# Scaling and splitting the value matrix of later batches on ScalarE and GpSimd, one fold for two column maxima, and another order of evictions near the last query block

## The chip, the cores and the metric

The kernel runs on one core of a Trainium2 chip. The metric is device time in microseconds (us). Engines as the profile names them: PE (TensorE, matrix products), PEld (its weight loads), DVE (VectorE), ACT (ScalarE), POOL (GpSimd), SP (SyncE, here only a DMA queue). Each engine executes its own instruction list in order and waits on semaphores of the others.

## The reference

Two layers run one after the other, all in float32.

1. Attention over pooled keys. For each of 4 batches, `kv` (384 x 32 positions, 128 channels) is averaged over 4 x 4 patches to 768 rows and multiplied with `w_sr`; the result is both `k` and `v`. For 12288 queries per batch: `s = q k^T / sqrt(128)`, softmax over the 768 keys, output `a v`.
2. A soft mixture of experts over all 49152 rows `x` of that output: `logits = x phi` (32 slots); a softmax over all rows (per slot) gathers slot inputs, 8 experts (128 to 1024 to 128, ReLU) map them, and a softmax over slots (per row) spreads the slot outputs back over the rows.

The queries and `phi` are scaled by 200, so the products need nearly full float32 accuracy: operands are split into a high and a low part and multiplied in several passes.

## The kernel before

**Tiling.** The queries are cut into 96 blocks of 512, 24 blocks per batch. For one block: `q_hi` (ACT, L448) and `q_lo` (POOL, L452) split the queries; `qk` (PE, L462 to L464) makes the scores of 768 keys in three PSUM pairs of banks (s0 to s2); `rowmax1` to `rowmax4` (DVE L469, L479, L481, a PE product L489, DVE L494, L499) find the row maximum and spread it; `sub` (DVE, L507) subtracts it and so frees the score banks; `exp_hi` and `exp_t` (ACT, L514, L518) make the exponentials as f16 and as f32; `plo` (POOL L523, on DVE for the last block) makes the low part of the f16 split; `av_hi` and `av_lo` (PE, L540, L541, L548) multiply with the value matrix; `av_evac` (L556 on DVE for block 94, the last but one, L558 on ACT for the others) moves the result out of one of two PSUM banks called m. Groups of 4 blocks then feed the softmax over rows of the second layer (`g0` to `g7a`, L582 to L685).

**The value matrix.** It is not `v` alone: `w_sb` holds `w_sr` and `w_sr phi` beside each other, so the matrix has 128 + 32 columns, and the logits come out of the same product. For each batch, `kv_ops` prepares it: `kv_k_*` (keys, split in two), `kv_v_mm` and `kv_v_out` (values, f32, tile `v32`), `kv_m` (DVE: largest absolute value in each row, for two halves h of the keys and for two column ranges k, 128 and 32 columns wide, L377; then L382 joins the halves), `kv_d` (ACT: puts those on a diagonal, L386), `kv_s_mm` and `kv_s_g` (PE and DVE: largest value over all rows, rounded down to a power of two, and its inverse), `kv_t_hi` (ACT L418: scaled values as f16, tile `vhi`), `kv_t_lo` (DVE: L425 sets the ones column of `vhi`, L426 makes `vlo = v * inv - vhi` in one instruction with two inputs in SBUF). For batch 0 this runs at the start; for batches 1 to 3 it runs in the last third of the batch before, between ordinary blocks.

**Order.** The order of all instructions on PE, DVE, ACT and POOL is written by the class `Plan`, a list scheduler. Each `op` gets an engine, an assumed cost, a priority (a planned time, smallest first), dependencies and the rings (tiles, PSUM banks) that it acquires and releases. `emit` simulates the engines with these assumed costs and calls the functions in simulated order; the chip's engines then keep that order, however long things really take. `PER` (9.8 us) is the assumed period of a block; the preparation of the next batch starts at the priority of `KV0` = 14.5 blocks after block 2 of a batch, and its steps lie `KVS` block periods apart. An `op` that releases a bank m gets 60 off its priority, so it comes first once it is ready. The plan assumed `dve(768) + 0.06` = 0.93 us and `dve(192) + 0.06` = 0.33 us for the two `kv_t_lo`.

**End.** After block 95, the last groups (L612 to L685), the experts (`t_psi` to `t_so`), the product `t_q` (L1063, PSUM bank m, tile `psq`) with its split `t_shi` and `t_slo`, and then chunks of output: `c_t`, `c_hi`, `c_lo` (a transposition through a bank m and its split), `o_mm`, `o_ev`, `o_dma`. The low parts of block 95 (`plo`, DVE) and the evictions of block 94 (`av_evac`, DVE) lie close together on DVE there.

Of the kernel before, what the change touches and what calls it, by code (L numbers as in the profile page):

```python
# [9 lines left out]
F32 = mybir.dt.float32  # L10
# [161 lines left out]
def attention_then_soft_moe(ctx: ExitStack, tc: tile.TileContext, qT, kv0, kvT, w_sr, w_srT, phi, w1, w2, outT):  # L172
# [112 lines left out]
    KVS = 0.9  # L285
# [84 lines left out]
    def kv_m(b, k, h):  # L370
        if k == 0 and h == 0:
            AM[b] = (
                bp.tile([P, 4], F32, tag="am", name=f"am_{b}", bufs=1),
                bp.tile([P, 2, P], F32, tag="dg", name=f"dg_{b}", bufs=1),
            )
        am = AM[b][0]
        nc.vector.tensor_reduce(  # L377
            out=am[:, 2 * h + k : 2 * h + k + 1], in_=VU[b][:, 3 * h : 3 * h + 3, VSRC[k]], axis=XY, op=ALU.max,
            apply_absolute_value=True,
        )  # L380
        if h:
            nc.vector.tensor_tensor(out=am[:, k : k + 1], in0=am[:, k : k + 1], in1=am[:, 2 + k : 3 + k], op=ALU.max)  # L382
# [25 lines left out]
    def kv_t_hi(b, k):  # L408
# [9 lines left out]
        nc.scalar.activation(hi[:, :, src.start + 1 : src.stop + 1], v[:, :, src], AF.Copy, scale=inv[:, k : k + 1])  # L418
# [131 lines left out]
    def av_evac(i, k):  # L550
# [4 lines left out]
        if i == NB - 2:  # L555
# [238 lines left out]
    def kv_ops(b, base, step, dep0, dep1):  # L794
# [11 lines left out]
        for h in range(2):  # L806
# [78 lines left out]
    def av_rest(i, k, m, p, prev):  # L885
        los = [ops["lo", i, 0], ops["lo", i, 1]]
        a2 = op("PE", 6 * 0.072, 0.17, p + 0.8, prev + los, lambda: av_lo(i, k), use=[("plo", (i, 0)), ("plo", (i, 1)), m])
        if k % 2:
# [4 lines left out]
                "DVE" if i == NB - 2 else "ACT", act(2 * VW) + (0.1 if i == NB - 2 else -0.03), 0.1, p - 2, [a2] + evs[-1:], lambda: av_evac(i, k // 2),  # L893
# [323 lines left out]
```

## Time and profile before

| what | value |
|---|---|
| median of 3 runs | 1143.38 us (1140.43 to 1143.49) |
| the profiled execution's own time | 1142.69 us |
| its span, first to last instruction | 1140.9 us |
| busy: PE, DVE, POOL, ACT | 1059.1, 1007.6, 860.3, 821.7 us |
| mean granted TensorE clock | 0.973 |

How to read it: busy time is a sum over an engine's instructions. In the lists of instructions a row gives start (us), duration (us), engine, line, operation and shapes, and in brackets the idle time just before it and what ended that. In lists of waits, a row gives who waited for whom, us in total, how often, and the longest. Rows of windows give, for a stretch of time, each engine's busy time with its instructions, the granted clock (PEclk), the DMA share and GB/s. L numbers are lines of the kernel before.

### The profile page before, as it was taken

How to read it: one execution, taken by the hardware profiler on the slowest of the kernel's cores; microseconds unless marked ns; L12 is line 12 of the kernel's file. 1: busy time of each engine (PE TensorE's matmuls, PEld its weight loads, DVE VectorE, ACT ScalarE, POOL GpSimd, SP SyncE). 2: the span in 40 equal slices, each digit the busy share in tenths (PEclk: the TensorE clock that was granted, in tenths of full speed). 3: DMA queues.
4: the chain of work that ended last, by engine and by line, in shares of the span. 5: the costliest groups of instructions: out<-in, count | busy, mean ns of one | idle time of the engine just before them, and what ended most of it. 6: DMA issues, size and time to landing. Idle time of an engine off the chain costs nothing.

```text
span 1140.9 us, 24642 instructions
## 1 busy us (share of the span) xinstructions
PE 1059.1 (93%) x10198; PEld 905.7 (79%) x10198; DVE 1007.6 (88%) x1506; ACT 821.7 (72%) x999; POOL 860.3 (75%) x471
## 2 busy tenths in 40 slices
PE   3799999998999999998999999998999999997785
PEld 2588888887888888887888888887888888886342
DVE  7889888999889988999989989999989988986895
ACT  1678778776777878776877788786788777874564
POOL 0678889777899889777889888868889889772430
PEclk9899999998999999999999999999999999998976
DMA  9225320120126310120136210210110110113398
GB/s 351 96 47 126 94 56 1 38 93 1 38 57 128 86 52 2 41 90 1 38 82 123 66 52 1 76 55 1 39 38 1 38 38 2 38 38 111 136 388 361
DMA packets 17406, 89.14 MB, mean 78 GB/s; under 512 B 1680, under 2 KB 3984, under 8 KB 11152
## 3 DMA queue, kind: packets, MB, share of 16 engines
q1 hardware_dynamic: 13408, 69.47, 16.4%
q0 software_dynamic: 3312, 17.70, 8.2%
q8 instruction: 81, 1.33, 0.5%
q10 hardware_dynamic: 576, 0.41, 0.1%
q14 instruction: 29, 0.24, 0.1%
HBM read 58.87 MB, written 25.17 MB: 74 GB/s over the span
## 4 chain that ended last, share of the span: by engine, by line
PE 63%; DVE 28%; issue 3%; ACT 2%; POOL 2%; DMA 1%; DVEq 0%; SPq 0%; POOLq 0%; ACTq 0%
PE m L540 10%; PE m L541 10%; PE m L548 9%; PE s L462 9%; DVE t L507 8%; PE s L464 8%; PE s L463 8%; DVE r L469 8%; PE m L489 3%; PE m L679 2%; DVE mb L499 2%; DVE o L1111 1%; POOL plo L523 1%; DVE cm L617 1%; PE po L1102 1%
## 5 line engine op out<-in xcount | busy, mean ns | idle before, releaser
L523 POOL TENSOR_TENSOR plo<-t,phi 128x1536 f16<-128x1536 f32 x190 | 595.4, 3144 | 153.8 <-ACT t L518 152.6
L514 ACT ACTIVATE phi<-t,lnk 128x1536 f16<-128x1536 f32 x192 | 301.0, 1570 | 120.2 <-DVE t L507 118.6
L469 DVE TRANSPOSE_TENSOR_REDUCE r<-s 128x32 f32<-128x1024 f32 x288 | 350.8, 1236 | 29.2 <-PE s L464 23.4
L540 PE MATMUL m<-vhi,phi 128*128 128x161 f16 x2280 | 358.3, 235 | 3.5 <-DVE acc L685 2.9
L541 PE MATMUL m<-vlo,phi 128*128 128x160 f16 x2280 | 357.5, 234 | 0.0
L507 DVE TENSOR_TENSOR t<-s,mb 128x1024 f32<-128x1024 f32 (+1 forms) x384 | 343.2, 951 | 8.2
L518 ACT ACTIVATE t<-t,lnk 128x1536 f32<-128x1536 f32 x192 | 299.7, 1568 | 2.8
L540 PEld LDWEIGHTS <-phi 128*128 128x128 f16 x2304 | 228.2, 99 | 24.7 <-issue 24.7
L462 PE MATMUL s<-qhi,khi 128*128 128x512 f32 x576 | 239.0, 415 | 5.8 <-DVE t L507 5.7
L541 PEld LDWEIGHTS <-phi 128*128 128x128 f16 x2304 | 226.7, 98 | 5.4 <-issue 3.9
L464 PE MATMUL s<-qhi,klo 128*128 128x512 f32 x576 | 229.3, 398 | 0.1
L463 PE MATMUL s<-qlo,khi 128*128 128x512 f32 x576 | 228.8, 397 | 0.0
L548 PE MATMUL m<-vhi,plo 128*128 128x161 f16 x2280 | 227.9, 235 | 0.2 <-POOL plo L523 0.2
L548 PEld LDWEIGHTS <-plo 128*128 128x128 f16 x2304 | 179.8, 101 | 2.6 <-issue 1.2
L558 ACT ACTIVATE xl<-m 128x322 f32<-128x322 f32 x188 | 81.0, 431 | 105.0 <-PE m L548 100.5
L452 POOL TENSOR_TENSOR qlo<-q,qhi 128x512 fp32r<-128x512 f32 x96 | 125.9, 1312 | 26.8 <-ACT qhi L448 26.8
L462 PEld LDWEIGHTS s<-qhi,khi 128*128 128x128 f32 x576 | 109.5, 190 | 29.8 <-issue 4.1
L464 PEld LDWEIGHTS s<-qhi,klo 128*128 128x128 f32 x576 | 109.1, 189 | 26.9 <-DVE klo L353 0.5
L463 PEld LDWEIGHTS s<-qlo,khi 128*128 128x128 f32 x576 | 109.6, 190 | 22.4 <-issue 0.7
L499 DVE STREAM_TRANSPOSE mb<-m 128x512 f32<-128x512 f32 x96 | 68.3, 711 | 3.3
L448 ACT ACTIVATE qhi<-q 128x512 fp32r<-128x512 f32 x96 | 59.1, 617 | 2.4 <-PE s L464 1.1
L489 PE MATMUL m<-rq,sel 128*128 128x64 f32 x192 | 40.5, 293 | 19.9 <-DVE rq L481 19.9
(136 smaller groups left out, 842.4 us busy)
## 6 DMA issues: line engine op xcount, KB each, us to landing
q<-qT SPq DMA_DIRECT2D x23, 1024.0 KB, 4.8
outT<-o SPq DMA_DIRECT2D x21, 1024.0 KB, 6.2
kva<-kvT POOLq DMA_DIRECT2D x9, 1536.0 KB, 11.6
kva<-kvT SPq DMA_DIRECT2D x3, 1536.0 KB, 10.2
kv<-kv SPq DMA_DIRECT2D x8, 512.0 KB, 5.7
w<-w SPq DMA_DIRECT2D x2, 1536.0 KB, 6.4
w<-w SPq DMA_DIRECT2D x4, 768.0 KB, 4.2
outT<-o SPq DMA_DIRECT2D x6, 512.0 KB, 6.2
```

Of the source, the lines that this page charges most:

```text
L452: nc.gpsimd.tensor_tensor(out=lo, in0=q_src(i), in1=hi.bitcast(F32), op=ALU.subtract)
L462: nc.tensor.matmul(s, khi[:, ks], hi, start=True, stop=False)
L463: nc.tensor.matmul(s, khi[:, ks], lo, start=False, stop=False)
L464: nc.tensor.matmul(s, klo[:, ks], hi, start=False, stop=True)
L469: nc.vector.tensor_reduce(out=MX[i][:, 2 * u : 2 * u + 2, :].rearrange("p t b -> p (t b)"), in_=S[i, u].rearrange("p t (b j) -> p (t b) j" ...
L507: nc.vector.tensor_tensor(out=TT_[i, h][:, o : o + n, :], in0=S[i, t // 2][:, u : u + n, :], in1=MX[i].unsqueeze(1).broadcast_to([P, n, BQ ...
L514: nc.scalar.activation(hi, TT_[i, h], AF.Exp, bias=lnk, scale=SCALE)
L518: nc.scalar.activation(t, t, AF.Exp, bias=lnk, scale=SCALE)
L523: eng.tensor_tensor(out=lo, in0=TT_.pop((i, h)), in1=PP[i, h], op=ALU.subtract)
L540: nc.tensor.matmul(px, p, vhi[:, t, :], start=(t == 0), stop=False)
L541: nc.tensor.matmul(px[:, 1:], p, vlo[:, t, :], start=False, stop=False)
L548: nc.tensor.matmul(px, PP[i, t // TH][1][:, t % TH, ks], vhi[:, t, :], start=False, stop=(t == NT - 1))
```

## The change

- `kv_m`: the four maxima lie as `[k, h]` in one tile, and one `tensor_reduce` over h writes both joined maxima to a new tile `am2`; the two `tensor_tensor` instructions of L382 go. `kv_d` reads `am2`, and both of its instructions come after all maxima.
- `kv_t_hi`, batches 1 to 3: ACT scales `v` in place (f32), then copies it to f16, two instructions in place of one for each column range. Batch 0 keeps its one.
- `kv_t_lo`, batches 1 to 3: POOL subtracts (`vlo = v - vhi`, v being scaled by now) and sets the ones column. Batch 0 keeps DVE.
- `av_evac` of block 94: its first half (query columns 0 to 255) stays on DVE, its second half goes from DVE to ACT. In the plan, the low parts of block 95 on DVE depend on that first half, so that it is written ahead of them.
- `t_q`: `psq` lies in the score banks s1 in place of a bank m.
- `KVS` from 0.9 to 1.0, and the plan's costs follow the new instructions.

```diff
-    KVS = 0.9
+    KVS = 1.0
...
-                bp.tile([P, 4], F32, tag="am", name=f"am_{b}", bufs=1),
+                bp.tile([P, 2, 2], F32, tag="am", name=f"am_{b}", bufs=1),
                 bp.tile([P, 2, P], F32, tag="dg", name=f"dg_{b}", bufs=1),
+                bp.tile([P, 2], F32, tag="am2", name=f"am2_{b}", bufs=1),
...
-            out=am[:, 2 * h + k : 2 * h + k + 1], in_=VU[b][:, 3 * h : 3 * h + 3, VSRC[k]], axis=XY, op=ALU.max,
+            out=am[:, k, h : h + 1], in_=VU[b][:, 3 * h : 3 * h + 3, VSRC[k]], axis=XY, op=ALU.max,
...
-        if h:
-            nc.vector.tensor_tensor(out=am[:, k : k + 1], in0=am[:, k : k + 1], in1=am[:, 2 + k : 3 + k], op=ALU.max)
+        if h and k:
+            nc.vector.tensor_reduce(out=am2, in_=am, axis=X, op=ALU.max)
...
-        nc.scalar.activation(dg[:, k, :], ident, AF.Copy, scale=am[:, k : k + 1])
+        nc.scalar.activation(dg[:, k, :], ident, AF.Copy, scale=am2[:, k : k + 1])
...
-        nc.scalar.activation(hi[:, :, src.start + 1 : src.stop + 1], v[:, :, src], AF.Copy, scale=inv[:, k : k + 1])
+        part = hi[:, :, src.start + 1 : src.stop + 1]
+        if b:
+            nc.scalar.activation(v[:, :, src], v[:, :, src], AF.Copy, scale=inv[:, k : k + 1])
+            nc.scalar.activation(part, v[:, :, src], AF.Copy)
+        else:
+            nc.scalar.activation(part, v[:, :, src], AF.Copy, scale=inv[:, k : k + 1])
...
+        if b:
+            if k == 0:
+                nc.gpsimd.memset(hi[:, :, :1], 1.0)
+            nc.gpsimd.tensor_tensor(out=lo[:, :, src], in0=v[:, :, src], in1=hi[:, :, src.start + 1 : src.stop + 1], op=ALU.subtract)
+            return
...
-        if i == NB - 2:
+        if i == NB - 2 and k == 0:
             nc.vector.tensor_copy(XL[g][:, o : o + 2, :], PX.pop((i, k)))
         else:
             nc.scalar.activation(XL[g][:, o : o + 2, :], PX.pop((i, k)), AF.Copy)
...
-            ops["lo", i, h] = op("DVE" if i == NB - 1 else "POOL", 1.67 if i == NB - 1 else 3.1, 0.1, T0 + 9 + 3.2 * h, [e2], lambda i=i, h=h: plo(i, h), acq=[("plo", (i, h))], use=[("t", (i, h)), ("phi", (i, h))])
+            ops["lo", i, h] = op(
+                "DVE" if i == NB - 1 else "POOL", 1.67 if i == NB - 1 else 3.1, 0.1, T0 + 9 + 3.2 * h,
+                [e2] + ([ops["x", NB - 2, 0]] if i == NB - 1 else []), lambda i=i, h=h: plo(i, h),
+                acq=[("plo", (i, h))], use=[("t", (i, h)), ("phi", (i, h))],
+            )
...
-            a = op("ACT", act(n, 1), 0.1, base + step * (6 + k), prev, lambda k=k: kv_t_hi(b, k), use=[("v32", b)])
-            ops["t", b, k] = op("DVE", dve(n) + 0.06, 0.08, base + step * (6 + k), [a], lambda k=k: kv_t_lo(b, k), use=[("v32", b)])
+            a = op("ACT", act(n, 1) * (2 if b else 1), 0.1, base + step * (6 + k), prev, lambda k=k: kv_t_hi(b, k), use=[("v32", b)])
+            ops["t", b, k] = op("POOL" if b else "DVE", 2.1 * n / 1000 + 0.3 if b else dve(n) + 0.06, 0.08, base + step * (6 + k), [a], lambda k=k: kv_t_lo(b, k), use=[("v32", b)])
...
-        W["psq"] = mt([P, 512], "psq")
+        W["psq"] = ps.tile([P, 2, 512], F32, tag="s1", name="psq")[:, 0, :]
```

More of the change, by code (lines that the diff above doesn't have):

```diff
@@ L372, in kv_m @@
             AM[b] = (
-                bp.tile([P, 4], F32, tag="am", name=f"am_{b}", bufs=1),
+                bp.tile([P, 2, 2], F32, tag="am", name=f"am_{b}", bufs=1),
                 bp.tile([P, 2, P], F32, tag="dg", name=f"dg_{b}", bufs=1),
+                bp.tile([P, 2], F32, tag="am2", name=f"am2_{b}", bufs=1),
             )
-        am = AM[b][0]
+        am, _, am2 = AM[b]
         nc.vector.tensor_reduce(
-            out=am[:, 2 * h + k : 2 * h + k + 1], in_=VU[b][:, 3 * h : 3 * h + 3, VSRC[k]], axis=XY, op=ALU.max,
+            out=am[:, k, h : h + 1], in_=VU[b][:, 3 * h : 3 * h + 3, VSRC[k]], axis=XY, op=ALU.max,
             apply_absolute_value=True,
         )
-        if h:
-            nc.vector.tensor_tensor(out=am[:, k : k + 1], in0=am[:, k : k + 1], in1=am[:, 2 + k : 3 + k], op=ALU.max)
+        if h and k:
+            nc.vector.tensor_reduce(out=am2, in_=am, axis=X, op=ALU.max)
     def kv_d(b, k):
-        am, dg = AM[b]
-        nc.scalar.activation(dg[:, k, :], ident, AF.Copy, scale=am[:, k : k + 1])
+        _, dg, am2 = AM[b]
+        nc.scalar.activation(dg[:, k, :], ident, AF.Copy, scale=am2[:, k : k + 1])
     def kv_s_mm(b):
@@ L812, in kv_ops @@
             for k in range(2):
-                m[k].append(op("DVE", (0.53 if k == 0 else 0.2) + 0.2 * h, 0.08, p + step * (1 + 0.4 * k), [at_["vo", h]] + m[k] + m[0][:1], lambda h=h, k=k: kv_m(b, k, h), use=[("v32", b)]))
-        d = [op("ACT", 0.25, 0.1, base + step * 5, m[k], lambda k=k: kv_d(b, k)) for k in range(2)]
+                m[k].append(op("DVE", (0.53 if k == 0 else 0.2) + 0.2 * h * k, 0.08, p + step * (1 + 0.4 * k), [at_["vo", h]] + m[k] + m[0][:1], lambda h=h, k=k: kv_m(b, k, h), use=[("v32", b)]))
+        d = [op("ACT", 0.4, 0.1, base + step * 5, m[0] + m[1], lambda k=k: kv_d(b, k)) for k in range(2)]
         s = op("PE", 0.6, 0.4, base + step * 5.5, d, lambda: kv_s_mm(b), acq=[("m", ("pa", b))])
@@ L892, in av_rest @@
             ops["x", i, k // 2] = op(
-                "DVE" if i == NB - 2 else "ACT", act(2 * VW) + (0.1 if i == NB - 2 else -0.03), 0.1, p - 2, [a2] + evs[-1:], lambda: av_evac(i, k // 2),
+                "DVE" if i == NB - 2 and k == 1 else "ACT", act(2 * VW) + (0.1 if i == NB - 2 and k == 1 else -0.03), 0.1, p - 2, [a2] + evs[-1:], lambda: av_evac(i, k // 2),
                 acq=[x] if first else [], use=[m] + ([] if first else [x]),
@@ L1148, in attention_then_soft_moe @@
         sq.append(tail("DVE", 1.05, [a] + sq, lambda h=h: t_so(h), use=[sk]))
-    a = tail("PE", 0.4, sq[1:], t_q, acq=[("m", "psq")])
-    shi = tail("ACT", 0.25, [a, qt], t_shi, use=[("m", "psq")])
-    slo = tail("DVE", 0.3, [shi], t_slo, use=[("m", "psq")])
+    a = tail("PE", 0.4, sq[1:], t_q, acq=[("s1", "psq")])
+    shi = tail("ACT", 0.25, [a, qt], t_shi, use=[("s1", "psq")])
+    slo = tail("DVE", 0.3, [shi], t_slo, use=[("s1", "psq")])
     for g in range(len(GB)):
```

## The prediction

> **What bounds the kernel now.** I read the page's busy times first, then the windows of equal length, then the waits of PE by stretch, and at last the lists of instructions around each wait.
>
> ```profile
> span 1140.9 us, 24642 instructions
> PE 1059.1 (93%) x10198; PEld 905.7 (79%) x10198; DVE 1007.6 (88%) x1506; ACT 821.7 (72%) x999; POOL 860.3 (75%) x471
> ```
>
> PE is the bound, DVE close behind. The average hides stages. Windows (columns: length, busy time and instructions of PE, PEld, DVE, ACT, POOL, clock, DMA):
>
> ```profile
> 313.70:342.20 28.50, 28.30 (x299) 24.92 (x297) 25.52 (x39) 21.10 (x25) 26.22 (x15) 1.00 0.30 57
> 256.70:285.20 28.50, 24.70 (x218) 22.19 (x216) 26.13 (x36) 18.54 (x24) 20.06 (x11) 0.88 0.01 1
> 770.00:798.60 28.60, 23.87 (x246) 20.85 (x245) 26.32 (x40) 18.96 (x24) 22.95 (x14) 1.00 0.00 1
> ```
>
> An ordinary window has PE busy throughout (28.30 of 28.50). The windows near the end of a batch, where the value matrix of the next one is prepared, have 24.70 and 23.87. PE time lost there is never made up, since PE has no slack elsewhere. What PE waited for, in the stretches 245 to 300 (the one from 500 to 560 reads the same), 755 to 815 (two rows), 196 to 257 (450 to 513 and 700 to 771 read the same), and last, for comparison, 795 to 1027, about 22 ordinary blocks:
>
> ```profile
> PE m L489 <- DVE rq L481: 3.8, 2, 3.1
> ...
> PE m L489 <- DVE rq L481: 4.4, 2, 3.1
> PE s L462 <- DVE t L507: 0.4, 1, 0.4
> ...
> PE m L679 <- DVE m L494: 1.0, 1, 1.0
> ...
> PE m L489 <- DVE rq L481: 0.9, 5, 0.2
> ```
>
> In 22 blocks together PE waits 0.9 us for the row maximum, and 3.1 us at once in each preparation. Why DVE is late there, with batch 0's two instructions of the same kind last:
>
> ```profile
> 255.67 3.12 POOL L523 TENSOR_TENSOR plo<-t,phi 128x1536 f16<-128x1536 f32 x1 [3.31 <-ACT t L518]
> 257.27 2.34 DVE L426 SCALAR_TENSOR_TENSOR vlo<-v,inv,vhi 128x768 f16<-128x768 f32 x1
> 259.99 3.09 POOL L523 TENSOR_TENSOR plo<-t,phi 128x1536 f16<-128x1536 f32 x1 [1.20 <-ACT t L518]
> 260.80 2.49 DVE L426 SCALAR_TENSOR_TENSOR vlo<-v,inv,vhi 128x192 f16<-128x192 f32 x1
> 263.93 0.66 PE L489 MATMUL m<-rq,sel 128*128 128x64 f32 x2 [3.12 <-DVE rq L481]
> 33.47 1.01 DVE L426 SCALAR_TENSOR_TENSOR vlo<-v,inv,vhi 128x768 f16<-128x768 f32 x1
> 34.40 0.41 DVE L426 SCALAR_TENSOR_TENSOR vlo<-v,inv,vhi 128x192 f16<-128x192 f32 x1
> ```
>
> The two instructions of L426 took 1.01 and 0.41 us at the start, where POOL ran nothing, and 2.34 and 2.49 beside `plo`. Each ends just after the POOL instruction beside it (258.79, 263.08), 0.8 and 0.2 us later. The small one is six times its own length. The plan had counted 0.93 and 0.33, so the order it wrote puts PE's row-maximum product 4.83 - 1.26 = 3.6 us too early, and PE stands for 3.1.
>
> **The price of the wait goes on in the clock.** After it PE runs slowly for a while (windows of 3 us):
>
> ```profile
> 264.00:267.00 3.00, 3.00 (x22) 3.00 (x23) 2.23 (x4) 0.00 (x0) 1.43 (x2) 0.50 0.00 0
> 267.00:270.00 3.00, 3.00 (x17) 2.71 (x15) 2.96 (x5) 2.78 (x3) 0.00 (x0) 0.52 0.00 0
> ...
> 518.00:521.00 3.00, 1.82 (x13) 1.85 (x14) 1.99 (x6) 0.00 (x0) 2.68 (x3) 0.67 0.00 0
> 521.00:524.00 3.00, 3.00 (x26) 2.86 (x24) 3.00 (x4) 1.63 (x2) 0.00 (x0) 0.76 0.00 0
> ```
>
> At clock 0.50 and 0.52 PE loses 3 x 0.50 + 3 x 0.48 = 2.9 us. In the second preparation it loses 3 x 0.33 + 3 x 0.24 = 1.7. In the third the clock stayed at 1.00 (window above): 4.6 us in all.
>
> **The change, part by part.**
>
> *Low parts and folds leave DVE.* Per later batch DVE loses both L426 (4.83 us) and both folds of L382, and gets one reduction over 4 numbers:
>
> ```profile
> L382 DVE TENSOR_TENSOR am<-am x8: 160/498/1506, 28.0 to 746.2; 128x1 f32<-128x1 f32 x8
> L619 DVE TENSOR_REDUCE cmt<-cm 128x1 f32<-128x16 f32 x23 | 3.9, 170 | 0.8
> ```
>
> L382 also has two SBUF inputs and takes 0.16 alone, up to 1.51 beside POOL. One such fold stands between PE's product L489 and L494, for which L679 then waits 1.0 us. The reduction has one input: nearest row 0.17, bounds 0.15 and 1.5 if it were held as well; I take 0.17, the mean of 23 of them, most of which ran while POOL was busy (it is 75% of the span). So the waits to go are 3.8 + 3.8 + 4.4 + 0.4 = 12.4, 3 x 1.0 = 3.0 and the clock's 4.6: 20.0 us. The Trainium skill, SBUF — State Buffer, section "SBUF: two separate sides", says that VectorE and GpSimd share a pair of ports as an exclusive lock for a whole instruction, and that on VectorE two SBUF inputs are enough to need it; by that rule the fold costs 0.17, without it up to 3 x 1.3 = 4 us of DVE would remain. The stretched L426 and L382 agree with it.
>
> *ACT and POOL get it.* The nearest rows:
>
> ```profile
> L418 ACT ACTIVATE vhi<-v,inv 128x768 f16<-128x768 f32 x4 | 3.7, 930 | 1.5 <-DVE inv L403 1.5
> L418 ACT ACTIVATE vhi<-v,inv 128x192 f16<-128x192 f32 x4 | 1.8, 444 | 0.0
> L523 POOL TENSOR_TENSOR plo<-t,phi 128x1536 f16<-128x1536 f32 x190 | 595.4, 3144 | 153.8 <-ACT t L518 152.6
> L227 POOL MEMSET sm<- 128x256 f32 x1 | 0.3, 315 | 0.0
> 270.89 3.13 POOL L523 TENSOR_TENSOR plo<-t,phi 128x1536 f16<-128x1536 f32 x1 [5.45 <-ACT t L518]
> ```
>
> ACT gets 0.93 + 0.44 = 1.37 us more per batch, and each copy waits for the scaling just ahead of it. Behind them on ACT stand exponentials and evictions, for which POOL's `plo` and PE's two m banks wait. POOL gets 3144 x 960 / 1536 = 1.97 us plus at most 0.32 for the ones column: 2.3. Behind it stand `plo` and `qlo`, for which PE waits. The cover: ACT is idle 7.4 us of the ordinary 28.5 above, and POOL waited 5.45 us for ACT near this place; the value matrix itself is needed some three blocks later. Bounds for both together: 0 (covered), and without cover all of it, 1.37 + 2.3 = 3.7 us per batch, 11 in all. I take 1.0 per batch, the size of the single PE wait above, so 3.0: nearer to the covered end. Transitions: 20.0 - 3.0 = 17.0 us. `KVS` 1.0 only spreads the same steps by half a block; the keys stay where they are, and the values have room: 0.
>
> *Evictions near the end.* On DVE, block 94's first eviction and the release of the other m bank stand behind block 95's first low part, which waits for ACT; PE waits for a bank:
>
> ```profile
> 1035.49 1.76 DVE L523 TENSOR_TENSOR plo<-t,phi 128x1536 f16<-128x1536 f32 x1 [2.27 <-ACT t L518]
> 1037.36 0.49 DVE L556 COPY xl<-m 128x322 f32<-128x322 f32 x1
> 1037.50 0.23 PE L540 MATMUL m<-vhi,phi 128*128 128x161 f16 x1 [2.88 <-DVE acc L685]
> 1039.58 0.34 PE L540 MATMUL m<-vhi,phi 128*128 128x161 f16 x1
> 1041.87 0.49 DVE L556 COPY xl<-m 128x322 f32<-128x322 f32 x1 [2.35 <-PE m L548]
> 1042.40 0.32 ACT L590 ACTIVATE xl<-xl,epk 128x12 f32<-128x12 f32 x1 [5.18 <-DVE xl L556]
> ```
>
> PE had ended the first half at 1037.50 - 2.88 = 1034.62. With the first eviction ahead of `plo`, DVE can do it then, in its 2.27 idle us, and PE goes on at 1035.2: 2.3 earlier. The half clock seen at 1039.58 (0.34 for 0.23) should not come after a 0.6 us wait: from 1037.85 to 1041.3 that is another 1.7. PE's last product of the block then ends near 1037.7 in place of 1041.7, ACT evicts it and goes on with L590 itself; DVE is through with both `plo` (1.76 each, from 1035.49) at 1039.0, and the next DVE step, which waited for L590 until 1042.40 + 0.32 = 1042.7, starts at 1039.05. Gain 3.7; bounds 0 (the clock and another bank take it) and 2.3 + 1.7 = 4.0. The chain from L590 to the experts has nothing beside it, so the output starts as much sooner.
>
> *psq.*
>
> ```profile
> 1065.37 2.74 DVE L1059 SCALAR_TENSOR_TENSOR so<-pso,mask,so 128x128 f32<-128x128 f32 x7
> 1068.76 0.49 PE L1063 MATMUL m<-so,sel 128*128 128x128 f32 x2 [1.30 <-DVE clo L1090]
> ```
>
> `so` is ready at 1068.11, the bank only at 1068.7: 0.6 us, bounds 0 and 0.65.
>
> *Sum.* 17.0 + 3.7 + 0.6 = 21.3. The profiled execution took 1142.69 us (span 1140.9), 0.7 below the median shown, so about 1121.4 by it and 1122.1 by the median. **I predict 1122 us.**
>
> **The rivals.**
>
> *B, the wait moves to ACT and POOL.* The doubled ACT work delays evictions and `plo`, and PE stands for those instead. For it: ACT's two pairs come between exponentials that POOL already waits for (152.6 us in the row of L523). Against it: the idle times above. At the uncovered price of 11 us in place of 3, the time is 1122 + 8 = 1130; if a wait grows past 3 us, the half clock comes back and it is 1132 to 1135. I put it at 1131.
>
> *C, moving work between DVE and POOL gains nothing.* A POOL subtraction of up to 1.6 us would hold up DVE's instructions as `plo` holds L426, so the transitions stay as they are and only the end gains 4.3: 1139. For it: L426 and L382 stretched. Against it: the remaining DVE instructions between L479 and L507 read PSUM and at most one SBUF tile, by the code. The Trainium skill, Perfetto Trace Analysis, section "Optimizing Scalar/DVE Operations", gives this as a warning: since GpSimd and VectorE share a port, offloading between them might not help. The rows bear it out for two-input instructions alone.
>
> *D, slower.* The place is PE's queue in ordinary blocks: the planner's new costs and the other `KVS` write another order for everything after the first preparation, some 80 blocks from block 16. A wait at L489 that recurs costs its length 80 times; from 21.3 / 80 = 0.27 us per block the kernel is not faster, at 0.35 it takes 1150. Against it: after each of the three preparations the order falls back into blocks that lose next to nothing (0.9 us in 22 blocks).
>
> *E, the change doesn't do what it says*, because PE would have waited for something else at the same place (score banks, L507): the transitions stay and the end gains, about 1139 as in C.
>
> **How the numbers follow.** Forecast 0.70 (its own range 1117 to 1128: from 20.0 + 4.6 gained, less nothing, to 15 gained), B 0.17, C and E together 0.08, D 0.05. The lower end of the range is the full sum and some 2 us for a better order elsewhere, 1116; the upper end takes in most of B, 1135. What is left out is C, D, E, the top of B and a rest below. 0.3% is 3.4 us, about what a measurement of this kernel can tell from no change. Faster: the forecast, B and a little of C and D, 0.89; the same: most of C and E, 0.07; slower: 0.04.
>
> **What would show it.** Right: no wait of PE at L489 above 1 us in the three preparations, clock 1.00 through them, PE busy above 28 us in such windows; POOL rows of about 1.6 and 0.4 us; no wait of 2.9 us of PE near block 95 and L590 some 3 to 4 us sooner after it; L1063 without its wait for `clo`. Wrong: PE waits at L540 for ACT's L558, or at L548 for POOL's `plo`, near the preparations (B); long DVE rows beside POOL's new ones (C); L489 waiting in ordinary blocks (D); L462 waiting for L507 (E).

## The result and the profile after

The kernel after took 1114.65 us (median of 4 runs, 1113.75 to 1116.73), the kernel before 1142.87 us beside it (1140.43 to 1143.49). The ratio is 0.976, with a 95% interval from 0.9739 to 0.978: 28.2 us, or 2.4%, faster. The forecast of 1122 us had the direction and most of the mechanism, but the time lies 1.35 us below the range.

The profiled execution took 1116.73 us. Line numbers grow by 11 for most of the loop: L489 is L500 after, L481 is L492, L494 is L505, L507 is L518, L523 is L534, L540 and L548 are L551 and L559, L679 is L690. L1063 is L1078. The page of after begins:

```profile
span 1115.0 us, 24632 instructions
PE 1050.2 (94%) x10198; PEld 903.4 (81%) x10198; DVE 985.8 (88%) x1492; ACT 823.1 (74%) x1006; POOL 866.0 (78%) x480
```

The span is 25.9 us shorter, but PE is busy 8.9 us less with the same 10198 products. Part of that is the half clock that went. The rest stayed unexplained until the experiments on addresses below.

Two windows where the value matrices of batches 1 and 3 are prepared (length, then PE, PEld, DVE, ACT, POOL, clock, DMA):

```profile
256.50:285.00 28.50, 27.37 (x289) 24.14 (x288) 25.49 (x44) 23.52 (x31) 27.33 (x18) 1.00 0.01 2
769.50:798.00 28.50, 28.50 (x303) 25.19 (x302) 24.92 (x35) 21.73 (x26) 24.04 (x12) 1.00 0.12 39
```

PE is busy 27.37 and 28.50 us there, where it had 24.70 and 23.87, and the clock is 1.00 in both. Of the prediction's sign "above 28 us" only the second window has it. PE's waits in the first preparation (196 to 300 us), in the second (440 to 560, two rows) and in the third (690 to 815, two rows); each row says who waited for whom, us in total, times, longest:

```profile
PE m L551 <- DVE m L505: 0.7, 1, 0.7
PE m L500 <- DVE rq L492: 0.7, 2, 0.4
...
PE m L500 <- DVE rq L492: 1.0, 3, 0.5
PE m L551 <- DVE m L505: 0.3, 1, 0.3
...
PE m L500 <- DVE rq L492: 0.9, 3, 0.4
PE m L551 <- DVE m L505: 0.3, 1, 0.3
```

The 3.1 us wait is gone in all three, and so is the 1.0 us wait of L690. What is left, 1.2 to 1.4 us per preparation, is still a wait for DVE. The new work on ACT, POOL and DVE, from the list of instructions:

```profile
258.33 0.92 ACT L421 ACTIVATE v<-v,inv 128x768 f32<-128x768 f32 x1
259.28 0.85 ACT L422 ACTIVATE vhi<-v 128x768 f16<-128x768 f32 x1
258.83 3.14 POOL L534 TENSOR_TENSOR plo<-t,phi 128x1536 f16<-128x1536 f32 x1
261.20 3.54 DVE L518 TENSOR_TENSOR t<-s,mb 128x1024 f32<-128x1024 f32 x4
261.87 0.16 POOL L432 MEMSET vhi<- 128x6 f16 x1
261.93 1.62 POOL L433 TENSOR_TENSOR vlo<-v,vhi 128x768 f16<-128x768 f32 x1
264.71 0.59 POOL L433 TENSOR_TENSOR vlo<-v,vhi 128x192 f16<-128x192 f32 x1
237.26 0.16 DVE L383 TENSOR_REDUCE am<-am 128x2 f32<-128x4 f32 x1
```

POOL's two subtractions take 1.62 and 0.59 us (1.57 and 0.39 were worked out), and DVE's four subtractions beside the large one take 3.54 us together, 0.89 each on average, where ordinary blocks of the same trace have 3.55: they are not held up. The reduction takes 0.16 us.

Near the end, block 94's first half is evicted in DVE's idle time, ahead of block 95's low parts. The last two rows are L590 and L595 of before:

```profile
1013.05 0.49 DVE L567 COPY xl<-m 128x322 f32<-128x322 f32 x1 [1.44 <-PE m L559]
1014.34 3.42 DVE L534 TENSOR_TENSOR plo<-t,phi 128x1536 f16<-128x1536 f32 x2
1016.34 0.44 ACT L569 ACTIVATE xl<-m 128x322 f32<-128x322 f32 x1 [0.77 <-PE m L559]
1016.81 0.32 ACT L601 ACTIVATE xl<-xl,epk 128x12 f32<-128x12 f32 x1
1017.68 0.22 DVE L606 RECIPROCAL r<-xl 128x12 f32<-128x12 f32 x1
```

L590 started at 1042.40, L601 starts at 1016.81: 25.6 us sooner, of which 4.0 are gained in this place, since block 95 itself came 21.6 us sooner. And `psq` now waits for its operand, not for a bank:

```profile
PE psq L1078 <- DVE so L1074: 0.8, 1, 0.8
```

A second view of the same two traces says where the time went. Block k is dated by DVE's transposition in it (L499 before, L510 after). The column gives by how much block k starts sooner after:

| place | sooner by, us | gained in it |
|---|---|---|
| block 2 | -1.8 | the start loses 1.8 |
| block 18 to 24, first preparation | -0.8 to 6.3 | 7.1 |
| 24 to 42, ordinary | 6.3 to 6.8 | 0.5 |
| 42 to 48, second preparation | 6.8 to 13.3 | 6.5 |
| 48 to 66, ordinary | 13.3 to 14.3 | 1.0 |
| 66 to 73, third preparation | 14.3 to 20.2 | 5.8 |
| 73 to 95, ordinary | 20.2 to 21.6 | 1.5 |
| 95 to the end | 21.6 to 25.9 | 4.3 |

The preparations give 19.4 us and the end 4.3. The start loses 1.8: a stretch of half clock that begins near 44 us lasts 6.8 us in this execution and lasted 3.4 in the one of before. But *ordinary* blocks gain too, some 0.05 us each. Nothing in the prediction did that.

### The profile page after: what moved, and what is told of

It is laid out like the page before. It is cut to its first block, busy times and chain, and to the rows that moved or that the text cites. A ratio compares the mean times of both kernels' runs of the same rounds, so it can differ in the third digit from the quotient of the medians.

```text
span 1115.0 us, 24632 instructions
## 1 busy us (share of the span) xinstructions
PE 1050.2 (94%) x10198; PEld 903.4 (81%) x10198; DVE 985.8 (88%) x1492; ACT 823.1 (74%) x1006; POOL 866.0 (78%) x480
## 4 chain that ended last, share of the span: by engine, by line
PE 70%; DVE 25%; ACT 2%; issue 1%; DMA 1%; POOL 1%; SPq 0%; DVEq 0%; ACTq 0%
PE m L551 11%; PE m L552 11%; PE m L559 10%; PE s L473 10%; PE s L475 9%; PE s L474 9%; DVE t L518 7%; DVE r L480 7%; PE m L500 3%; PE m L690 2%; PE po L1117 2%; DVE mb L510 2%; DVE cm L628 1%; DVE o L1126 1%; DVE pool L311 1%
## 5 line engine op out<-in xcount | busy, mean ns | idle before, releaser
L534 POOL TENSOR_TENSOR plo<-t,phi 128x1536 f16<-128x1536 f32 x190 | 595.9, 3148 | 125.5 <-ACT t L529 125.1
L551 PE MATMUL m<-vhi,phi 128*128 128x161 f16 x2280 | 354.8, 234 | 2.5 <-DVE m L505 1.3
L552 PE MATMUL m<-vlo,phi 128*128 128x160 f16 x2280 | 353.9, 233 | 0.0
L518 DVE TENSOR_TENSOR t<-s,mb 128x1024 f32<-128x1024 f32 (+1 forms) x384 | 343.1, 950 | 8.8 <-DVE mb L510 0.9
L551 PEld LDWEIGHTS <-phi 128*128 128x128 f16 x2304 | 226.7, 99 | 22.9 <-issue 22.8
L559 PE MATMUL m<-vhi,plo 128*128 128x161 f16 x2280 | 226.8, 234 | 0.2 <-POOL plo L534 0.2
L559 PEld LDWEIGHTS <-plo 128*128 128x128 f16 x2304 | 178.5, 100 | 1.2 <-issue 0.6
L510 DVE STREAM_TRANSPOSE mb<-m 128x512 f32<-128x512 f32 x96 | 68.3, 711 | 3.3
L505 DVE TENSOR_REDUCE m<-m 128x16 f32<-128x64 f32 x96 | 21.5, 224 | 40.3 <-PE m L500 40.3
```

The costliest lines, as they stand in the source:

```text
L518: nc.vector.tensor_tensor(out=TT_[i, h][:, o : o + n, :], in0=S[i, t // 2][:, u : u + n, :], in1=MX[i].unsqueeze(1).broadcast_to([P, n, BQ ...
L534: eng.tensor_tensor(out=lo, in0=TT_.pop((i, h)), in1=PP[i, h], op=ALU.subtract)
L551: nc.tensor.matmul(px, p, vhi[:, t, :], start=(t == 0), stop=False)
L552: nc.tensor.matmul(px[:, 1:], p, vlo[:, t, :], start=False, stop=False)
L559: nc.tensor.matmul(px, PP[i, t // TH][1][:, t % TH, ks], vhi[:, t, :], start=False, stop=(t == NT - 1))
```

## The experiments

Times are medians in us. The kernel before ran beside each of them: 1142.69 with e1 to e4, 1142.25 with e5 to e8, 1142.33 with e9 to e12, and one run each, 1142.76 with f1 to f4 and 1141.08 with g1 and g2. The first question was the ordinary blocks, the second what each part of the change is worth. Line numbers in a run's rows are those of its own kernel; names of tiles and operations tell which instruction it is. Where a diff is shortened, `...` stands for what is left out.

### Ordinary blocks: the same work in another place

Between the traces of before and after, one group of instructions differs everywhere: the score products. In the groups of 80 to 200 us (busy us, mean ns of one, idle before), three rows of before and then three of after:

```profile
L462 PE MATMUL s<-qhi,khi 128*128 128x512 f32 x69 | 28.6, 415 | 0.0
L463 PE MATMUL s<-qlo,khi 128*128 128x512 f32 x69 | 27.2, 395 | 0.0
L464 PE MATMUL s<-qhi,klo 128*128 128x512 f32 x68 | 26.9, 396 | 0.0
```

```profile
L473 PE MATMUL s<-qhi,khi 128*128 128x512 f32 x70 | 28.8, 411 | 0.0
L475 PE MATMUL s<-qhi,klo 128*128 128x512 f32 x70 | 27.4, 391 | 0.0
L474 PE MATMUL s<-qlo,khi 128*128 128x512 f32 x69 | 26.9, 390 | 0.0
```

They are 4 to 6 ns shorter, while the value products have 234 and 233 ns in both. From start to start of successive score products (blocks 4 to 93, gaps under 0.29 us) the mean is 0.2330 us before and 0.2285 after. Nobody touched these products. What did change is where their operands lie. The new tile `am2` has 8 bytes and takes a slot of 32, so every tile allocated behind it moved up by 32 bytes. The built programs put the first `qhi` at 142496 (before) and at 142528 (after); `khi` and `klo` stayed.

**e1: the kernel before, with no edit**, to see how far two profiles of one kernel differ.

> The kernel before, unchanged, for a second profile. Between the profiles of before and after, ordinary blocks (no preparation of the next batch in them) became 0.08 us shorter each, 3.9 us in all, with the same instructions; the three score products follow each other at 0.2330 us before and 0.2287 after. Theory A (addresses): the new tile of 8 bytes moved all later tiles in SBUF by 32 bytes, and TensorE reads them faster; then this run shows 0.233 again. Theory B (another execution or chip): TensorE was a little faster in that profile; then this run may show anything from 0.2287 to 0.233. The start (two blocks) lost 1.8 us between the profiles; if that is only the phase of the half-clock windows, the start differs here too by up to 1.7 us.

One run, 1145.36 us. The spacing is 0.2330 again. The three preparations differ from the first profile by the length of the half clock after the 3.1 us wait: 3.4, 6.8 and 3.4 us, where it was 6.8, 3.4 and none.

**e2: before, with after's addresses.**

```diff
-                bp.tile([P, 4], F32, tag="am", name=f"am_{b}", bufs=1),
+                bp.tile([P, 16], F32, tag="am", name=f"am_{b}", bufs=1),
```

> The kernel before with 48 unused bytes added to the tile of the maxima, so that every later SBUF tile lies 32 bytes further, where the changed kernel has it; no instruction differs. Theory A (addresses): score products at 0.2287 us, ordinary blocks 0.08 us shorter, the whole 4 to 7 us faster than before (ratio 0.994 to 0.9965). Theory B (execution or chip): no difference, ratio 1.000 within 0.001, spacing as in the second profile of before.

1137.25 (1136.35 to 1138.31), ratio 0.9951 [0.9938, 0.9964]: 5.4 us faster for a tile that nobody reads more of.

```profile
L462 PE MATMUL s<-qhi,khi 128*128 128x512 f32 x70 | 28.8, 411 | 0.0
```

**e3: after, with before's addresses** (`am2` as columns 4 and 5 of `am`, which stays in one 32-byte slot).

```diff
-                bp.tile([P, 2, 2], F32, tag="am", name=f"am_{b}", bufs=1),
+                bp.tile([P, 8], F32, tag="am", name=f"am_{b}", bufs=1),
...
-                bp.tile([P, 2], F32, tag="am2", name=f"am2_{b}", bufs=1),
...
+        am, am2 = am4[:, :4].rearrange("p (k h) -> p k h", k=2), am4[:, 4:6]
...
```

> The changed kernel with both joined maxima in the tile of the maxima itself, so that later tiles keep the addresses that they had before; instructions as in the changed kernel. Theory A (addresses): 4 to 7 us slower than the changed kernel, 1118 to 1121 us (ratio to before 0.978 to 0.981), score products at 0.233. Theory B: as the changed kernel, about 1114.7 us (0.975 to 0.976).

1120.42 (1119.85 to 1122.54), ratio 0.9807 [0.9791, 0.9822]: 5.8 us slower than after. The mean period of an ordinary block (57 of them, outside the preparations) says the same twice: 10.213 us before and 10.150 in e2, with its addresses moved; 10.160 after and 10.224 in e3, with its addresses moved back. That is 0.063 and 0.064 us a block, 5.8 in 92.

**e8: before, moved by 64 bytes** (`am` with 96 bytes).

```diff
-                bp.tile([P, 4], F32, tag="am", name=f"am_{b}", bufs=1),
+                bp.tile([P, 24], F32, tag="am", name=f"am_{b}", bufs=1),
```

> The kernel before with the tile of the maxima 64 bytes larger, so that the split queries lie at 142560 in place of 142496 bytes; at 142528 the kernel was 5.4 us faster. Theory of 64-byte multiples (142528 is one, 142496 and 142560 are not): no gain, 1142.7, score products at 0.233 us. Theory of any other place (banks or distances of the tiles): 1137, products at 0.229.

1142.46, ratio 1.0009 [0.9998, 1.002], spacing 0.2331. So it isn't that `am` is larger. At this point, multiples of 64 bytes fitted everything.

**e12: after, with the rows of `vhi` padded to 384 bytes**, to give the value products the same good.

```diff
-                bp.tile([P, NT, VW], F16, tag="vhi", name=f"vhi_{b}"),
+                bp.tile([P, NT, 192], F16, tag="vhi", name=f"vhi_{b}")[:, :, :VW],
```

> The kernel after, with the rows of vhi padded from 161 to 192 float16 elements, so that each moving row of the value products L551 and L559 starts at a multiple of 64 bytes; the padding is not read and qhi stays at a multiple of 64. Theory A (the 64-byte effect that made the 512-column score products 1.8% quicker holds for these products as well): up to 3 us faster than after, about 1112 us. Theory B (it holds only for the score products): 1114.7 us, no change beyond 0.3%.

1120.05 (1119.34 to 1120.56), ratio 0.9807 [0.9794, 0.9821]: 5.4 us *slower* than after. The value products kept their 234 and 233 ns, and the score products were back at the slow mean, though `qhi` lay at 143232, a multiple of 64:

```profile
L473 PE MATMUL s<-qhi,khi 128*128 128x512 f32 x69 | 28.7, 415 | 0.0
```

So the simple rule fell. It stayed open which tile's address it is, and modulo what.

**f1 and f2: `qhi` and `qlo` alone moved by 32 bytes**, in before and in after. Each q tile becomes 128 bytes longer, so tiles behind them move by 512.

```diff
-            qp.tile([P, BQ], F32R, tag="qhi", name=f"qhi_{i}", bufs=2),
-            qp.tile([P, BQ], F32R, tag="qlo", name=f"qlo_{i}", bufs=2),
+            qp.tile([P, BQ + 32], F32R, tag="qhi", name=f"qhi_{i}", bufs=2)[:, 8 : 8 + BQ],
+            qp.tile([P, BQ + 32], F32R, tag="qlo", name=f"qlo_{i}", bufs=2)[:, 8 : 8 + BQ],
```

> The kernel before, with the score products' moving tiles qhi and qlo alone moved by 32 bytes (142528, as in after), all later tiles moved by 512 bytes, so that they stand to multiples of 128, 256 and 512 bytes as in before. Theory A (the address of the moving rows decides, whatever lies elsewhere): the spacing of the 512-column products falls from 0.233 to 0.229 us and the time to about 1137 us. Theory B (another tile's address decides, or how q stands to it): 0.233 us and about 1142 us.

> The kernel after, with qhi and qlo alone moved by 32 bytes (to 142560, 96 above a multiple of 128), all later tiles moved by 512 bytes. Theory A (the address of the moving rows decides): the spacing goes back to 0.233 us and the time to about 1120 us. Theory B (another tile's address): 0.229 us and 1114.7 us.

f1 took 1137.96 us, f2 1120.79, one run each. f2 is as expected of the q address: spacing 0.2337. f1 is more telling. Its mean of 0.2304 lies halfway, because even and odd blocks use two pairs of tiles, which the longer tiles put 2176 bytes apart: even blocks have 0.2282 us, odd ones 0.2326. In the groups of two stretches of 5 us of f1, first an odd block (31), then an even one (32):

```profile
L464 PE MATMUL s<-qhi,klo 128*128 128x512 f32 x6 | 2.4, 395 | 0.0
L463 PE MATMUL s<-qlo,khi 128*128 128x512 f32 x6 | 2.4, 393 | 0.0
...
L464 PE MATMUL s<-qhi,klo 128*128 128x512 f32 x6 | 2.3, 390 | 0.0
L463 PE MATMUL s<-qlo,khi 128*128 128x512 f32 x6 | 2.3, 389 | 0.0
```

Within one program the two kinds of blocks differ, for these products, in the address of the moving operand. In before, where both pairs stand alike to multiples of 256 bytes, even and odd blocks have 0.2329 and 0.2330 us, so that they are even or odd makes no difference by itself.

**f3 and f4: before, moved by 96 and by 160 bytes** (the second line is f4's).

```diff
+                bp.tile([P, 32], F32, tag="am", name=f"am_{b}", bufs=1),
+                bp.tile([P, 48], F32, tag="am", name=f"am_{b}", bufs=1),
```

> The kernel before, with all tiles behind the small tile am moved by 96 bytes: qhi at 142592, a multiple of 128. Theory A (a multiple of 64 is enough): 0.229 us and about 1137 us. Theory B (as the padded vhi suggests, whose qhi lay at a multiple of 128: it takes 64 above a multiple of 128): 0.233 us and about 1142 us.

> The kernel before, with all tiles behind the small tile am moved by 160 bytes: qhi at 142656, 64 above a multiple of 128 and of 256 (in after it is 64 above a multiple of 128 and 192 above one of 256). Theory A (64 above a multiple of 128): 0.229 us and about 1137 us. Theory B (192 above a multiple of 256, or something other than q's address): 0.233 us and about 1142 us.

f3: spacing 0.2295, 1141.08 us in its one run. f4: 0.2328, 1145.95. Both expectations of "64 above a multiple of 128" fell, one on each side. Single runs of before lie between 1139.88 and 1146.13, so here the spacing is the evidence and not the time.

**g1 and g2: q at the multiples of 64 not yet tried.** In g1, even blocks have q at 0 and odd ones at 128 above a multiple of 256; in g2 at 192 and at 64. The q tiles are 128 bytes longer, and `am` is longer (first line g1, second g2):

```diff
+                bp.tile([P, 96], F32, tag="am", name=f"am_{b}", bufs=1),
+                bp.tile([P, 80], F32, tag="am", name=f"am_{b}", bufs=1),
...
+            qp.tile([P, BQ + 32], F32R, tag="qhi", name=f"qhi_{i}", bufs=2)[:, :BQ],
+            qp.tile([P, BQ + 32], F32R, tag="qlo", name=f"qlo_{i}", bufs=2)[:, :BQ],
```

> The kernel before with qhi and qlo of even blocks at a multiple of 256 bytes (142848, 147200) and of odd blocks 128 above one (145024, 149376). Addresses so far: with q 192 (142528, 146880) and 0 (142592) above a multiple of 256 the spacing was 0.2282 to 0.2296 us, with 64, 96, 128, 160 and 224 above it was 0.2326 to 0.2341. Theory A (the moving rows' address modulo 256 decides: 0 and 192 quick): even blocks 0.229 to 0.230, odd blocks 0.233, and about 1140 us. Theory B (modulo 512, or q's place against another tile): even blocks 0.233 too.

> The kernel before with qhi and qlo of even blocks 192 above a multiple of 256 bytes (qhi at 142784, which is 448 above one of 512, where the quick ones so far were 192 above one of 512) and of odd blocks 64 above one (144960, 149312). Theory A (modulo 256): even blocks 0.228 to 0.229 us, odd blocks 0.233, and about 1140 us. Theory B (modulo 512, or q's place against another tile): even blocks 0.233 too, about 1142.5 us.

Even blocks 0.2297 and 0.2285, odd blocks 0.2332 and 0.2326: as theory A said, four times. The times are single runs, 1141.21 and 1140.56. All addresses together:

| q tiles above a multiple of 256 bytes | spacing, us | seen in |
|---|---|---|
| 0 | 0.2295, 0.2297 | f3, g1 even |
| 192 | 0.2285, 0.2285, 0.2282, 0.2285 | after, e2, f1 even, g2 even |
| 64 | 0.2328, 0.2326, 0.2326 | f4, f1 odd, g2 odd |
| 128 | 0.2333, 0.2332 | e12, g1 odd |
| 160 | 0.2330 | before |
| 224 | 0.2331, 0.2332 | e8, f2 even |
| 96 | 0.2341 | f2 odd |

### What each part is worth

**e4: the fold alone** (one reduction for the two joins, the plan's costs for it, `KVS` 0.9, old addresses).

```diff
...
-        if h:
-            nc.vector.tensor_tensor(out=am[:, k : k + 1], in0=am[:, k : k + 1], in1=am[:, 2 + k : 3 + k], op=ALU.max)
+        if h and k:
+            nc.vector.tensor_reduce(out=am2, in_=am, axis=X, op=ALU.max)
...
```

> The kernel before with only the fold changed (one reduction with one input for both maxima, its costs in the plan); low parts stay on DVE, addresses as before, steps at 0.9. The predicted share: 3 x 1.0 us (the wait of the group product for the row maximum), so 1140 us. From the two profiles, the blocks in which folds stand became 1.8 us shorter in each preparation: theory of more (the fold delays every row maximum behind it): 5.3 us, 1137.6. Rival: the stretching of the folds is hidden by DVE's idle time: no difference, 1142.9.

1140.22 (10 runs), ratio 0.9978 [0.9967, 0.999]: 2.5 us. The 1.0 us wait of the group product (L679 of before) goes, the wait for `rq` stays, here in the first preparation:

```profile
PE m L491 <- DVE rq L483: 4.3, 3, 3.1
```

**e5: scaling and low parts alone** (ACT and POOL for batches 1 to 3, with the plan's costs for them, `KVS` 0.9, old addresses).

```diff
...
+            nc.scalar.activation(v[:, :, src], v[:, :, src], AF.Copy, scale=inv[:, k : k + 1])
+            nc.scalar.activation(part, v[:, :, src], AF.Copy)
...
+            nc.gpsimd.tensor_tensor(out=lo[:, :, src], in0=v[:, :, src], in1=hi[:, :, src.start + 1 : src.stop + 1], op=ALU.subtract)
+            return
...
```

> The kernel before with only the scaling and the low parts of batches 1 to 3 moved to ScalarE and GpSimd, with their costs in the plan; folds, steps at 0.9, evictions, psq and addresses as before. The theory of the prediction: the wait of 3.1 us of TensorE in each preparation and the half clock after it go, 12.4 + 4.6 = 17.0 us, less up to 3.0 for the new work: 1126 to 1129 us (ratio 0.985 to 0.988). From the block times of the changed kernel at the old addresses (4.3 us gained in the block with the low parts, and about 1 in the next): 15 to 16 us, 1127. Rival (the folds and the low parts only work together): less than 10 us.

1133.31 (1132.83 to 1134.43), ratio 0.993 [0.9917, 0.9943]: 8.9 us, less than expected. The longest wait falls from 3.1 to 1.2 us and no half clock follows, but in each preparation 2.7 to 3.1 us of waits remain. PE's waits in the first one:

```profile
PE m L499 <- DVE rq L491: 2.0, 4, 1.2
PE m L689 <- DVE m L504: 1.0, 1, 1.0
```

DVE's fold, which here is still the one with two inputs, stands ahead of the row maximum for which L689, the group product of this kernel, waits. In the list of instructions (start, duration):

```profile
238.62 1.50 DVE L382 TENSOR_TENSOR am<-am 128x1 f32<-128x1 f32 x1
```

**e6: only the plan told the truth.** The prediction had blamed the order as well: the plan counted 0.93 and 0.33 us for instructions of 2.4.

```diff
-            ops["t", b, k] = op("DVE", dve(n) + 0.06, 0.08, base + step * (6 + k), [a], lambda k=k: kv_t_lo(b, k), use=[("v32", b)])
+            ops["t", b, k] = op("DVE", 2.4 if b else dve(n) + 0.06, 0.08, base + step * (6 + k), [a], lambda k=k: kv_t_lo(b, k), use=[("v32", b)])
```

> The kernel before with one number changed: the plan counts 2.4 us for each low part on DVE in batches 1 to 3, in place of 0.93 and 0.33; the instructions stay on DVE and stay stretched beside GpSimd. Theory P (the order was written for the wrong length, TensorE's row-maximum product stands too early): with the right length the planner puts other products ahead of it and the wait of 3.1 us shrinks to under 1.5; 6 to 12 us gained, 1131 to 1137 us. Theory D (DVE is full there, whatever the order): the wait only moves to another place, under 3 us gained, 1140 to 1143.

1143.6, ratio 1.001 [0.9999, 1.0022]: nothing. The 3.1 us wait goes, and others take its place, in each preparation alike:

```profile
PE s L462 <- DVE t L507: 2.4, 1, 2.4
PE m L489 <- DVE rq L481: 1.3, 3, 0.7
PE m L679 <- DVE m L494: 1.0, 1, 1.0
PE m L540 <- ACT xl L558: 0.5, 1, 0.5
```

The half clock follows the wait of 2.4 us as well: 3.4, 6.8 and 3.4 us in the three preparations. Ahead of the first of these waits DVE is busy 13.41 of the 14 us from 262 to 276. DVE is nearly full there, and this other order only chose which of PE's products waits.

**e7: the end alone** (block 94's evictions, the low parts' dependency, `psq`).

```diff
-        if i == NB - 2:
+        if i == NB - 2 and k == 0:
...
+                [e2] + ([ops["x", NB - 2, 0]] if i == NB - 1 else []), lambda i=i, h=h: plo(i, h),
...
+        W["psq"] = ps.tile([P, 2, 512], F32, tag="s1", name="psq")[:, 0, :]
```

> The kernel before with only the evictions of block 94, the plan's dependency of block 95's low parts on the first of them, and psq in the score banks; addresses as before. By the prediction's terms 3.7 + 0.6 = 4.3 us: 1138.4 us (ratio 0.996). Rival (the output at the end is bound by its transfers, which end when they end): under 1 us gained.

1138.73 (10 runs), ratio 0.9971 [0.9959, 0.9982]: 3.5 us. Its profile has blocks up to 95 unchanged and everything behind 5.0 us sooner.

**e9: low parts and fold together**, the edits of e4 and e5 in one kernel.

> The kernel before with two parts together: scaling and low parts of batches 1 to 3 on ScalarE and GpSimd, and the column maxima folded with one input; the plan counts the steps as before (0.9), the evictions near the end, psq and the addresses stay. Each part alone gave 8.9 us (1142.3 to 1133.3) and 2.5 us (1142.7 to 1140.2). Theory A (the parts add up): 1142.3 - 8.9 - 2.5 = 1131 us. Theory B (the fold takes VectorE out of the 1.0 us for which TensorE still waited at the L689 product with the low parts alone, and so opens up the rest): 1126 to 1127 us, and that wait of 1.0 is gone in all three preparations.

1127.68 (1124.47 to 1128.91), ratio 0.9869 [0.9851, 0.9887]: 14.7 us, where the parts add up to 11.4. By the medians the fold is worth 5.6 us on top of the low parts and 2.5 by itself, and theory B was nearer, 1 us short. The waits that remain in the first preparation (the third has 1.9 in place of 1.7):

```profile
PE m L501 <- DVE rq L493: 1.7, 2, 1.2
```

The traces don't show that the two parts help each other. The 19 blocks of the preparations (18 to 24, 42 to 48, 66 to 73) take 219.7 us in before, 215.4 in e4, 207.4 in e5 and 203.9 in e9: the fold saves 4.3 us by itself and 3.5 behind the low parts, the low parts 12.4. What the medians have beyond that lies elsewhere. From block 95 to the end, where these four kernels have the same instructions, the traces have 113.0, 114.2, 115.3 and 111.8 us. Why e5 is slow there stays open.

**e10: after, with `KVS` back at 0.9.**

```diff
-    KVS = 1.0
+    KVS = 0.9
```

> The kernel after, with the plan's spacing of preparation steps put back from 1.0 to 0.9; all else as in after. Theory A (the spacing is worth something, since with 0.9 and the low parts alone TensorE still waited 2.0 + 1.0 us in each preparation for VectorE): 1117 to 1119 us against after's 1114.7. Theory B (the spacing is worth nothing, as the prediction had it): 1114 to 1115.5 us.

1117.64 (1117.34 to 1117.75), ratio 0.9785 [0.9772, 0.9798]: 3.0 us slower than after. PE waits for `rq` 2.0, 2.3 and 2.3 us in the three preparations, where after has 0.7, 1.0 and 0.9:

```profile
PE m L500 <- DVE rq L492: 2.0, 3, 1.2
```

So the wider spacing of the same steps is worth about 1 us per batch. The 19 blocks of the preparations say 2.4 for all three, 202.7 us against 200.3. What DVE does ahead of the row maximum for which PE waits 1.2 us isn't the preparation's:

```profile
263.63 0.65 DVE L701 TENSOR_REDUCE RM<-LL 128x16 f32<-128x512 f32 x1
264.20 0.70 DVE L628 TRANSPOSE_TENSOR_REDUCE cm<-LL 128x16 f32<-128x512 f32 x1
268.29 0.32 DVE L490 TENSOR_REDUCE m<-r 128x16 f32<-128x96 f32 x1 [0.28 <-ACT xl L569]
```

L701 and L628 belong to a group's softmax over rows; with four small ones of the same group they put 2.1 us between the block's readings of its scores and L490. After has L701 and L628 at 258.92 and 260.41, ahead of its block's subtraction (261.20). The spacing gave the plan another order, and this one is better.

**e11: after, with each POOL subtraction done four times.**

```diff
             nc.gpsimd.tensor_tensor(out=lo[:, :, src], in0=v[:, :, src], in1=hi[:, :, src.start + 1 : src.stop + 1], op=ALU.subtract)
+            nc.gpsimd.tensor_tensor(out=lo[:, :, src], in0=v[:, :, src], in1=hi[:, :, src.start + 1 : src.stop + 1], op=ALU.subtract)
+            nc.gpsimd.tensor_tensor(out=lo[:, :, src], in0=v[:, :, src], in1=hi[:, :, src.start + 1 : src.stop + 1], op=ALU.subtract)
+            nc.gpsimd.tensor_tensor(out=lo[:, :, src], in0=v[:, :, src], in1=hi[:, :, src.start + 1 : src.stop + 1], op=ALU.subtract)
```

> The kernel after, with each GpSimd subtraction of the low parts done four times over, the output unchanged: 3 x (1.62 + 0.59) = 6.6 us more of GpSimd for each of the three batches, 20 us in all. Theory A (GpSimd's new work lies behind TensorE's own): less than 1.5 us slower than after, 1114.7 to 1116.2 us. Theory B (rival B of the prediction: the ordinary blocks' low parts on GpSimd come late and TensorE waits for them): up to 6 us for each batch, 1130 us or more, with waits of TensorE for the eviction chain's plo in these windows.

1127.66 (1127.3 to 1130.69), ratio 0.9879 [0.9863, 0.9895]: 13.0 us slower for 19.9 us of POOL. The cover that the prediction named does not hold this much. First preparation, from the list of instructions:

```profile
265.77 1.57 POOL L436 TENSOR_TENSOR vlo<-v,vhi 128x768 f16<-128x768 f32 x1
270.90 3.11 POOL L537 TENSOR_TENSOR plo<-t,phi 128x1536 f16<-128x1536 f32 x1
274.04 1.82 DVE L521 TENSOR_TENSOR t<-s,mb 128x512 f32<-128x512 f32 x2 [2.46 <-POOL plo L537]
274.88 0.47 PE L476 MATMUL s<-qhi,khi 128*128 128x512 f32 x1 [1.78 <-DVE t L521]
```

PE's waits in it:

```profile
PE m L503 <- DVE rq L495: 2.7, 3, 2.0
PE s L476 <- DVE t L521: 1.8, 1, 1.8
PE m L554 <- DVE m L508: 0.7, 1, 0.7
```

The path is not the one that rival B named. A late `plo` (270.90 here, 266.38 after) holds the tile `t`; DVE, which subtracts into `t`, waits 2.46 us for it, and so PE waits for the score banks that this subtraction frees. In the second and third preparation this wait is 2.3 and 2.6 us, and 3.4 us of half clock follow each. Together PE's waits grow by 9.0 us (12.9 in the three preparations, 3.9 in after), and the half clock costs some 3.4: that makes 12.4 of the 13.0. How much more work POOL could take for nothing, this one point can't say.

### The sum of the parts

| step | median, us | worth |
|---|---|---|
| before | 1142.33 | |
| + low parts (e5, with 1142.25 beside it) | 1133.31 | 8.9 |
| + fold (e9) | 1127.68 | 5.6 |
| + end and addresses (e10) | 1117.64 | 10.0 |
| + `KVS` 1.0 (after) | 1114.65 | 3.0 |

The end and the addresses measured by themselves are 3.5 and 5.4 to 5.8, 8.9 to 9.3 of the 10.0. The rest, about 1 us, isn't assigned. For the other steps the blocks of the preparations are the better measure, since start and end, and with them the medians, also vary with the half clock: 12.4 us for the low parts, 3.5 for the fold and 2.4 for `KVS`, 18.3 in all. e3, with all three at the old addresses, has 201.4 us there, 18.3 less than before. The 19.4 us that after gains there hold 1.2 more for its addresses, 19 blocks of 0.063 us.

## Why the prediction was right, and where it wasn't

**What bounds the kernel: right.** PE, and in the preparations DVE's instructions with two SBUF inputs beside POOL. e9 takes these away and gets 14.7 us.

**Transitions, 20.0 less 3.0: right in sum, not in its parts.** The medians give 8.9 + 5.6 + 3.0 = 17.5 for low parts, fold and `KVS`, the blocks of the preparations 12.4 + 3.5 + 2.4 = 18.3, against 17.0. That the sum is so near is in part luck: the low parts were to bring 12.4 + 4.6 - 3.0 = 14.0 and brought 12.4 (8.9 by the medians), and `KVS`, put at nothing, made it up. The waits went as forecast: 12.4 us, at L489 but for 0.4, became 0.7 + 1.0 + 0.9 = 2.6 in stretches that are longer, the three of 1.0 went, and the clock stayed at 1.00. The 3.0 set aside for ACT's and POOL's new work does not appear as waits for them: the 3.9 us that PE still waits in the three preparations are all for DVE's `rq` and `m`.

**The fold, 0.17 us: right**, 0.16 measured, against 1.50 in e5 with the old form. The Trainium skill, SBUF — State Buffer, section "SBUF: two separate sides" (exclusive lock, needed on VectorE by two SBUF inputs), agrees with both numbers. Its worth was taken as the three waits of 1.0 us. In the preparations it is 4.3 alone and 3.5 behind the low parts.

**`KVS`, "0": wrong, 3.0 us.** The step that failed is "`KVS` 1.0 only spreads the same steps by half a block". It also gives the plan another order of the group instructions beside them, and at 0.9 (e10) PE waits 1.2 us at once for `rq` in each preparation.

**"The order it wrote puts PE's row-maximum product 3.6 us too early": half right.** The numbers hold, but with the true costs in the plan (e6) the time stays. Both causes name the same instructions; of the two ways tried, only taking them away helped.

**The end, 3.7 + 0.6: right.** 4.0 us at L601, 4.3 to the end by the traces of before and after, 3.5 by the medians of e7 and 5.0 by its trace. `psq` waits for `so` alone.

**The step that failed: the sum has no term for addresses.** It ran 17.0 + 3.7 + 0.6. The change also adds a tile of 8 bytes, and this moved the moving operand of 1728 products to a quicker address: 5.4 us by e2, 5.8 by e3 against after. At the old addresses the changed kernel takes 1120.42 us, 1.6 from the forecast and inside the likeliest case's own range (whose lower end of 1117 is a little low for its parts: 1142.69 - 24.6 = 1118.1). In the profile before, no row told that 0.2330 us from product to product could be less.

**The rivals.** B did not happen (POOL's 2.4 us per batch are covered), though e11 shows that the cover ends: 6.6 us more per batch cost 4.3. C fell: moving the low parts from DVE to POOL, with their scaling on ACT, gained 8.9 us, and DVE's rows beside POOL's new ones keep their length (0.89 us). The warning in the Trainium skill, Perfetto Trace Analysis, section "Optimizing Scalar/DVE Operations", that offloading between the two might not help, did not come true here, where the instructions that moved had two SBUF inputs on DVE. D fell: the ordinary block of e3, with the new order and the old addresses, has 10.224 us against 10.213, 0.011 us where 0.27 were needed. E's wait (L462 for L507) is not in after. It is what e6 and e11 run into.

## What to carry to other kernels

When two engines stretch each other's instructions, price the stretch and take away the instruction: another order, planned with true costs, moved the wait and gained nothing. Measure a part in the stretch where it works: by medians of a few runs the fold seemed worth 2.5 us alone and 5.6 behind the low parts, by the blocks of the preparations 4.3 and 3.5. And after any change to the list of tiles, compare the mean duration of products that nobody touched: here the move that an 8-byte tile caused was worth 5.4 us, a fifth of the whole gain.

## What the runs showed of the hardware that was not expected

**The address of a moving operand.** With float32r rows of 512 columns (2048 bytes), products follow each other at 0.2282 to 0.2297 us when the row starts 0 or 192 bytes above a multiple of 256, and at 0.2326 to 0.2341 when it starts 64, 96, 128, 160 or 224 above one. Since the tiles `khi` and `klo` lay 192 above a multiple of 256 in all these kernels, the runs can't say whether it is the address itself or its distance from the weights'; 32 wasn't tried. Padding `vhi` to rows of 384 bytes left the value products as they were.

**The half clock after a wait varies.** After the same 3.1 us wait it lasted 6.8, 3.4 and 0 us in the three preparations of one execution of before, and 3.4, 6.8 and 3.4 in another (e1). Shorter waits can bring it too: 2.4 us (e6) brought 3.4, 6.8 and 3.4, and 2.3 and 2.6 us (e11) brought 3.4 each. Waits of 1.2 us (e5, e9) and of 1.8 and 2.0 us, 7 us apart (e11, first preparation), brought none.
